# The first chunk of a fused attention and feed-forward kernel rebuilt: two load queues for z, z casts on GpSimd, split z copies, first units squared in halves

## Chip, cores, metric

One NeuronCore of a Trainium2 chip (the sets of rounds ran on four chips; ratios compare runs of one set). The metric is the device time of one execution in microseconds (us). Each figure is the median of several runs. Executions of one program here scatter by about 0.3% (the kernel before: 1205.06 to 1208.82 us in its first four runs), and part of this study is about where that scatter comes from. The record lists a state with every run: those that are compared here are all listed as "fast", or, for a single run, as unknown.

Names of engines: PE is TensorE (PEld its weight loads), DVE is VectorE, ACT is ScalarE, POOL is GpSimd (called Pool below), SP is SyncE.

## The reference

```python
def _attn_ref(u, v, z):                       # u, v: (8, 3008, 256), z: (8, 3008, 64)
    scores = np.matmul(z, z.transpose(0, 2, 1)) / S
    attn = np.maximum(scores, 0.0) ** 2
    return (u * np.matmul(attn, v)).astype(np.float32)

def _moe_ref(x, w_in, w_out):                 # x: (24064, 256), d_ff 2048
    h = x @ w_in
    g = h * (1.0 / (1.0 + np.exp(-1.702 * h)))
    return (g @ w_out).astype(np.float32)     # the kernel's output
```

The attention has no softmax: scores are rectified and squared.

## The kernel before

One batch follows another. For each batch, the 3008 rows are taken in 6 chunks of 512 queries. A *unit* is two blocks of 128 keys against one chunk: two score matmuls into a 128x1024 PSUM tile `sc`, a rectification into `rl`, a square into `a`. An *output step* is one matmul of a V block with half a unit, into one of two accumulators `o`. The first chunk of the first batch has 47 output steps (48 matmuls, since one step has two matmuls of 64 rows); steps 4k to 4k+3 need unit k. Nothing runs ahead of that chunk, so here the whole latency from the first load is bare. Later batches get z by transposing DMAs; the first batch turns z on TensorE instead, in six *turns* of four blocks:

```python
    def first_cast(g):                        # f32 -> f16, written twice (two row halves)
        m = g % CB * CB
        for c in range(2):
            dve.tensor_copy(ZT["st"][g // CB][:, m:m + CB, c, :], ZT["f"][g // CB][:, m:m + CB, :])

    def first_zt(g):
        z2 = ZT["st"][g // CB][:, g % CB * CB:(g % CB + 1) * CB]
        zp = ps1.tile([P, CB, P], F16, name="zp", tag="ps1")       # PSUM
        for k in range(CB):
            pe.transpose(zp[:, k, :], z2[:, k, :, :], ident)
        # ... cut: dst and src views of ZT and zp
        if g in (0, 2, 3):
            act.activation(dst, src, AF.Copy, scale=1.0)
        else:
            dve.tensor_copy(dst, src)
        # ... cut: the odd block of the last turn, copied by VectorE

    def square(b, i, jp, sc):                 # ... cut: forms of later batches
        rl = pw.tile([P, 2, CH], F16, name="rl", tag="rl", bufs=3)
        act.activation(rl, sc, AF.Relu, scale=csc)
        a = pa.tile([P, 2, CH], F16, name="a", tag="a", bufs=21)
        dve.tensor_tensor(a, rl, rl, ALU.mult)
        # ... cut: transposing DMA of a for a later chunk
```

The start of the program, and when units of the first chunk are taken (step: number of units):

```python
    FIRST_ZT = {2: 2, 7: 3, 13: 4, 21: NCH - 1}                  # step: turn
    SCHED0 = {0: {0: 1, 6: 2, 14: 2, 22: 2, 30: 2, 38: 2}, # ... cut: later chunks

    load_v(0, 0, act)                         # V loads; the casts of V run on Pool
    first_z((0, CB, 2 * CB, 4 * CB, NJ))      # all z loads on SP, in four pieces
    for n0 in range(VB, NJ, VB):
        load_v(0, n0, sp)
    warm_up(7)                                # matmuls on nothing
    first_cast(0)
    first_zt(0)
    warm_up(2)
    first_cast(1)
    posts = scores(0, [queue.pop(0) for _ in range(2)])
    first_zt(1)
    posts[0]()                                # a post is one square(...)
    first_cast(2)
    posts[1]()
    first_cast(3)
    take(0, 1)
```

In the traces here each engine works its instructions off in the order of the program: below, a z cast starts at 14.33, right behind the four squares queued ahead of it. A framework adds the semaphore waits from the tiles that the instructions read and write.

## Time and profile before

| | before |
|---|---|
| time, median (range) of the first three runs | 1206.41 us (1205.06 to 1208.82) |
| span of the profiled run | 1203.2 us |
| TensorE busy in 0 to 10, 10 to 20, 20 to 30 us | 6.97, 7.00, 10.00 us |
| first scores | 5.45 us |
| first output matmul | 8.57 us |
| *marker*: first output matmul of the second chunk | 26.91 us |

The page of the profile, its first lines (busy us of each engine, share of the span, instructions):

```profile
span 1203.2 us, 28259 instructions
...
PE 1190.2 (99%) x11785; PEld 715.2 (59%) x11785; DVE 830.5 (69%) x1277; ACT 770.5 (64%) x903; POOL 307.1 (26%) x363
```

Busy time by stretch of the kernel before. The columns are the stretch in us, its length, then each engine's busy us with the number of its instructions, the granted clock of TensorE, the busy share of the DMA engines and GB/s:

```profile
0.00:10.00 10.00, 6.97 (x35) 2.37 (x35) 4.57 (x12) 5.41 (x6) 2.46 (x9) 1.00 0.76 232
10.00:20.00 10.00, 7.00 (x45) 2.73 (x44) 9.06 (x14) 5.94 (x8) 9.77 (x14) 1.00 1.18 277
20.00:30.00 10.00, 10.00 (x52) 3.43 (x51) 7.72 (x11) 7.84 (x9) 2.58 (x4) 1.00 1.23 167
```

TensorE is the limit from 20 us on. Before that it idles 3.03 us in the first stretch and 3.00 us in the second. Of its 6.97 busy us in the first, 3.71 are warm-up matmuls (3.12 and 0.59 us in the timeline), so these are no work either.

The timeline of the kernel before (start us, busy us, engine, line, operation, output and input tiles, shape, count, and in brackets the idle time before with what ended it):

```profile
3.81 0.49 DVE L123 CAST zst<-zf 128x256 f16<-128x256 f32 x2 [2.68 <-DMA zf<-in_z_dram]
...
4.36 0.40 PE L129 MATMUL zp<-ident,zst 128*128 128x128 f16 x4
...
4.80 0.60 ACT L135 ACTIVATE ZT<-zp 128x512 f16<-128x512 f16 x1 [2.26 <-PE zp L129]
...
5.45 0.61 PE L217 MATMUL sc<-ZT 64*128 64x512 f16 x4 [0.26 <-ACT ZT L135]
...
5.88 1.94 ACT L231 ACTIVATE rl<-sc 128x1024 f16<-128x1024 f32 x2 [0.49 <-PE sc L217]
...
7.84 0.68 DVE L245 TENSOR_TENSOR a<-rl 128x1024 f16<-128x1024 f16 x1
...
8.57 0.59 PE L304 MATMUL o<-a,V 128*128 128x512 f16 x2
...
14.33 1.31 DVE L123 CAST zst<-zf 128x256 f16<-128x256 f32 x2
...
15.70 0.40 PE L129 MATMUL zp<-ident,zst 128*128 128x128 f16 x4 [2.35 <-DVE zst L123]
...
24.11 2.33 PE L304 MATMUL o<-a,V 128*128 128x512 f16 x10
...
26.91 1.90 PE L304 MATMUL o<-tt,V 128*128 128x512 f16 x8
```

The chain of the first unit is cast, turn, copy, scores, rectification, square, output. The 2.35 us at 15.70 is the largest wait: a cast of z stands in VectorE's queue behind four squares.

### The profile page before, as it was taken

The page shows a single profiled execution, that of the slowest core. Times are in us where ns is not written, and L with a number is a line of the kernel's source. Part 1 is how long each engine was busy: PE and PEld are TensorE (multiplying, and loading weights), DVE is VectorE, ACT ScalarE, POOL GpSimd, SP SyncE. Part 2 cuts the span into 40 slices and gives each one's busy share as a digit, 9 for nine tenths or more (in the row PEclk, how much of TensorE's full clock was granted, in tenths as well). Part 3 has the DMA queues.
Part 4 walks back from the last instruction along what each step waited for, and adds up shares of the span by engine and source line. Part 5 has one row for each costly group of instructions (what it writes and reads, how often), then busy time and mean ns, then how long its engine had stood idle before and what let it go on. Part 6 is the DMA issues. An engine that isn't in the chain of part 4 may idle for free.

```text
span 1203.2 us, 28259 instructions
## 1 busy us (share of the span) xinstructions
PE 1190.2 (99%) x11785; PEld 715.2 (59%) x11785; DVE 830.5 (69%) x1277; ACT 770.5 (64%) x903; POOL 307.1 (26%) x363
## 2 busy tenths in 40 slices
PE   7999999999999999999999999999999999999998
PEld 2446765467644676446765468554775547844577
DVE  7669954597545976469654696648966489564886
ACT  6777684476844768366683666736677376772764
POOL 4144300352004520044200451015510134101000
PEclk9999999999999999999999999999999999999999
DMA  9966399562994639844399454984459754496012
GB/s 225 169 112 129 114 168 158 86 153 72 169 161 89 151 91 174 159 78 137 94 186 146 80 137 98 194 133 76 138 121 183 133 83 149 114 180 117 1 37 71
DMA packets 366592, 152.33 MB, mean 127 GB/s; under 512 B 313312, under 2 KB 358496, under 8 KB 366464
## 3 DMA queue, kind: packets, MB, share of 16 engines
q1 hardware_dynamic: 330320, 114.08, 48.6%
q0 software_dynamic: 35456, 35.86, 14.8%
q8 instruction: 92, 1.51, 0.5%
q10 hardware_dynamic: 688, 0.59, 0.2%
q14 instruction: 36, 0.29, 0.1%
HBM read 60.29 MB, written 24.64 MB: 71 GB/s over the span
## 4 chain that ended last, share of the span: by engine, by line
PE 95%; DMA 2%; DVE 2%; ACT 1%; issue 0%; SPq 0%; ACTq 0%; DVEq 0%
PE o L304 37%; PE hg L345 26%; PE st L445 17%; PE yp L511 8%; PE sc L217 6%; DMA tt<-a 2%; DVE a L245 1%; ACT rl L231 0%; DMA zf<-in_z_dram 0%; DVE gt L354 0%; DVE zst L123 0%; ACT gf L353 0%; DVE s L416 0%; DVE s L418 0%; PE zp L129 0%
## 5 line engine op out<-in xcount | busy, mean ns | idle before, releaser
L353 ACT ACTIVATE gf<-hg 128x1024 f32<-128x1024 f32 (+1 forms) x384 | 385.8, 1007 | 166.0 <-PE hg L345 138.8
L231 ACT ACTIVATE rl<-sc 128x1024 f16<-128x1024 f32 x311 | 308.1, 1025 | 208.0 <-PE sc L217 205.9
L304 PEld LDWEIGHTS <-V 64*128 64x128 f16 (+1 forms) x4052 | 233.9, 94 | 251.4 <-issue 10.0
L345 PE MATMUL hg<-xt,W 128*128 128x512 f16 (+1 forms) x1408 | 354.5, 374 | 0.1
L354 DVE TENSOR_SCALAR gt<-gf 128x1024 f16<-128x1024 f32 (+1 forms) x384 | 275.5, 718 | 89.0 <-ACT gf L353 84.7
L245 DVE TENSOR_TENSOR a<-rl 128x1024 f16<-128x1024 f16 x276 | 192.0, 697 | 183.8 <-ACT rl L231 181.0
L304 PE MATMUL o<-a,V 64*128 64x512 f16 (+2 forms) x2010 | 316.4, 372 | 0.0
L187 POOL DMA_DIRECT2D uq<-in_u_dram x188 | 129.6, 696 | 509.2 <-PE sc L217 343.5
L304 PE MATMUL o<-tt,V 64*128 64x512 f16 (+1 forms) x1762 | 215.3, 376 | 2.0 <-DMA tt<-a 2.0
L345 PEld LDWEIGHTS <-W 128*128 128x128 f16 x1536 | 141.2, 98 | 117.5 <-issue 0.3
L445 PEld LDWEIGHTS <-gt 128*128 128x128 f16 x2176 | 132.5, 98 | 29.8 <-issue 1.1
L217 PE MATMUL sc<-ZT 64*128 64x512 f16 (+1 forms) x692 | 121.3, 366 | 1.9 <-ACT ZT L135 0.9
L445 PEld LDWEIGHTS <-s 128*128 128x128 f16 x1632 | 99.2, 98 | 20.7
L172 POOL CAST V<-vst 128x512 f16<-128x512 f32 x96 | 90.2, 978 | 65.3 <-DMA vst<-in_v_dram 58.3
L511 PE MATMUL yp<-W,gt 64*128 64x256 f16 x1664 | 104.0, 269 | 0.0
L511 PEld LDWEIGHTS <-gt 64*128 64x128 f16 x1664 | 80.7, 94 | 19.0 <-POOLq L84 4.1
L321 DVE TENSOR_TENSOR xt<-o,ut 128x512 f16<-128x512 f32 x80 | 51.5, 685 | 38.1 <-PE o L304 38.1
L445 PE MATMUL st<-WT,gt 128*128 128x128 f16 x1088 | 71.8, 219 | 0.9 <-ACT uP L455 0.9
L445 PE MATMUL st<-W,gt 128*128 128x128 f16 x1088 | 71.7, 219 | 0.0
L445 PE MATMUL st<-WT,s 128*128 128x128 f16 x1088 | 71.5, 219 | 0.0
L455 ACT ACTIVATE uP<-st 128x256 f32<-128x256 f32 x102 | 39.1, 383 | 38.4 <-DVE y L461 33.7
L217 PEld LDWEIGHTS <-ZT 64*128 64x128 f16 x692 | 37.5, 94 | 37.7 <-issue 6.8
(47 smaller groups left out, 627.3 us busy)
## 6 DMA issues: line engine op xcount, KB each, us to landing
vst<-in_v_dram SPq DMA_DIRECT2D x39, 512.0 KB, 5.0
uq<-in_u_dram POOLq DMA_DIRECT2D x156, 128.0 KB, 3.4
out_dram<-y SPq DMA_DIRECT2D x33, 512.0 KB, 3.7
tt<-a SPq DMA_TRANSPOSE x230, 3.6
uq<-in_u_dram POOLq DMA_DIRECT2D x32, 112.0 KB, 2.9
out_dram<-y POOLq DMA_DIRECT2D x7, 512.0 KB, 5.0
vst<-in_v_dram SPq DMA_DIRECT2D x8, 384.0 KB, 4.5
out_dram<-y POOLq DMA_DIRECT2D x7, 384.0 KB, 4.6
```

The source lines that it names most:

```text
L172: pool.tensor_copy(V16[b][:, n0:n0 + VB, k, :].rearrange("p n (q c) -> p n q c", c=QW), vst.rearrange("p n (q k c) -> p n q k c", k=NCC, c ...
L187: eng.dma_start(uq[k * QW:(k + 1) * QW, :n // QW].rearrange("t q k c -> t q (k c)"), src[:, :, cs])
L217: pe.matmul(sc[:, r, :m * P], zt[h, 2 * kp + r, :], zt[h, (qi + 1) * CB - m:(qi + 1) * CB, :], start=True, stop=True,)
L231: act.activation(rl, sc, AF.Relu, scale=csc)
L245: dve.tensor_tensor(a, rl, rl, ALU.mult)
L304: ins = pe.matmul(acc[c][:, :n], V16[b][h, j, c, :], weights(b, i, j)[h], start=(k, m) == first[c], stop=(k, m) == final[c],)
L321: dve.tensor_tensor(x[:, c, :n], acc[c][:, :n], ut[:, :n], ALU.mult)
L345: pe.matmul(hg[:, e, :n], W1[:, c, ff * P:(ff + 1) * P], XT[b, i][:, c, :n], start=(c == 0), stop=(c == NCC - 1),)
L353: act.activation(gf[:, :, :n], hg[:, :, :n], AF.Gelu_apprx_sigmoid, scale=1.0 / FSC)
L354: dve.tensor_scalar(g, gf[:, :, :n], FSC, None, ALU.mult)
L445: pe.matmul(bank[:, m, :], lhs()[:, f, m, :], right[:, ff, :], start=name in ("P1", "P2", "P5") and m == 0 and ff == 0, stop=ff == NFF // ...
L511: ins = pe.matmul(yp[s // per][:, s % per, :], GT[b, k, ff // CB][h, ff % CB, s * P:(s + 1) * P], W2[h, ff, :], start=new, stop=n == last[ ...
```

## The change

The intent, as its parts show it: bring the second z piece and the first V blocks earlier (z on two queues, V loads reordered), take the z casts off the busy VectorE (to Pool), shorten the first chain by splitting z copies and units between ScalarE and VectorE, and take units every 7 steps, each time with one z turn.

The core of the diff, cut. The new order of loads and of casts on Pool:

```diff
-    load_v(0, 0, act)
-    first_z((0, CB, 2 * CB, 4 * CB, NJ))
-    for n0 in range(VB, NJ, VB):
-        load_v(0, n0, sp)
+    first_z(0, CB, sp)
+    first_z(CB, 2 * CB, act)
+    casts = load_v(0, 0, act)
+    first_z(2 * CB, 4 * CB, sp)
+    for n0 in (VB, 2 * VB):
+        casts += load_v(0, n0, sp)
+    first_z(4 * CB, NJ, sp)
+    for n0 in range(3 * VB, NJ, VB):
+        casts += load_v(0, n0, sp)
+    first_cast(0, pool, 0, 1)
+    for n, cast in enumerate(casts):
+        if n in (0, 4, 8, 9):
+            first_cast((0, 4, 8, 9).index(n) + 2, pool)
+        cast()
     warm_up(7)
+    first_cast(0, dve, 1, 2)
+    first_cast(1, dve)
```

Split copies, halves of units, and the first two units:

```diff
+            act.activation(dst[:, :SREM], src[:, :SREM], AF.Copy, scale=1.0)
+            dve.tensor_copy(dst[:, SREM:], src[:, SREM:])
...
+    def square_halves(jp, sc, r_dve):
+        rl = pw.tile([P, 2, CH], F16, name="rl", tag="rl", bufs=3)
+        a = unit[0, 0, jp] = pa.tile([P, 2, CH], F16, name="a", tag="a", bufs=21)
+        for r in range(2):
+            if r in r_dve:
+                dve.tensor_scalar(rl[:, r], sc[:, r], csc, 0.0, ALU.mult, ALU.max)
+            else:
+                act.activation(rl[:, r], sc[:, r], AF.Relu, scale=csc)
+        for r in range(2):
+            dve.tensor_tensor(a[:, r], rl[:, r], rl[:, r], ALU.mult)
+        turn_unit(0, 0, jp, a)
...
+    FIRST = {7: (2, 3), 14: (2, 4), 21: (2, 5), 28: (2,), 35: (2,), 42: (1,)}   # step: units, turn
+    HALVES = {2: (), 3: (0,), 5: (0,), 7: (0,), 9: (0,)}     # unit: halves rectified by VectorE
...
+    copies = first_zt(2)
+    rls = [pw.tile([P, 2, CH], F16, name="rl", tag="rl", bufs=3) for _ in range(2)]
+    for k, r in ((0, 0), (0, 1), (1, 1)):
+        act.activation(rls[k][:, r], scs[k][:, r], AF.Relu, scale=csc)
+    dve.tensor_scalar(rls[1][:, 0], scs[1][:, 0], csc, 0.0, ALU.mult, ALU.max)
+    for k in range(2):
+        a = unit[0, 0, k] = pa.tile([P, 2, CH], F16, name="a", tag="a", bufs=21)
+        for r in range(2):
+            dve.tensor_tensor(a[:, r], rls[k][:, r], rls[k][:, r], ALU.mult)
+    copies()
```

More of the change, by code (lines that the diff above doesn't have):

```diff
@@ L96, in warm_up @@
             pe.matmul(w, nil[:, :P], nil, start=(k == 0), stop=(k == n - 1))
-    def first_z(cuts):
-        ZT[0] = pz.tile([P, NJ, P], F16, name="ZT", tag="ZT")
-        ZT["st"] = [pa.tile([P, CB * CB, 2, DQK], F16, name="zst", tag="tt", bufs=14) for _ in range(2)]
-        fs = [pw.tile([P, CB * CB, DQK], F32, name="zf", tag="y") for _ in range(2)]
-        for n0, n1 in zip(cuts, cuts[1:]):
-            zf = fs[n0 // (CB * CB)]
-            m0 = n0 % (CB * CB)
-            t0, last = n0 * P, n1 == NJ
-            t1 = (n1 - CB if last else n1) * P
-            sp.dma_start(
-                zf[:, m0:m0 + (t1 - t0) // P, :].rearrange("p (g n) d -> p g (n d)", n=CB),
-                z[0, t0:t1].rearrange("(g p n) d -> p g (n d)", p=P, n=CB),
-            )
-            if last:
-                m1 = m0 + (t1 - t0) // P
-                sp.dma_start(zf[:, m1:m1 + CB - 1, :], z[0, t1:S0].rearrange("(p n) d -> p n d", n=CB - 1))
-                for h in range(2):
-                    sp.dma_start(zf[h * SREM:(h + 1) * SREM, m1 + CB - 1, :], z[0, S0:S])
-        ZT["f"] = fs
@@ L120, in first_cast, with first_z @@
-    def first_cast(g):
+    def first_z(n0, n1, eng):
+        if 0 not in ZT:
+            ZT[0] = pz.tile([P, NJ, P], F16, name="ZT", tag="ZT")
+            ZT["st"] = [pa.tile([P, CB * CB, 2, DQK], F16, name="zst", tag="tt", bufs=14) for _ in range(2)]
+            ZT["f"] = [pw.tile([P, CB * CB, DQK], F32, name="zf", tag="y") for _ in range(2)]
+        zf = ZT["f"][n0 // (CB * CB)]
+        m0 = n0 % (CB * CB)
+        t0, last = n0 * P, n1 == NJ
+        t1 = (n1 - CB if last else n1) * P
+        eng.dma_start(
+            zf[:, m0:m0 + (t1 - t0) // P, :].rearrange("p (g n) d -> p g (n d)", n=CB),
+            z[0, t0:t1].rearrange("(g p n) d -> p g (n d)", p=P, n=CB),
+        )
+        if last:
+            m1 = m0 + (t1 - t0) // P
+            eng.dma_start(zf[:, m1:m1 + CB - 1, :], z[0, t1:S0].rearrange("(p n) d -> p n d", n=CB - 1))
+            for h in range(2):
+                eng.dma_start(zf[h * SREM:(h + 1) * SREM, m1 + CB - 1, :], z[0, S0:S])
@@ L121, in first_cast @@
+    def first_cast(g, eng, c0=0, c1=2):
         m = g % CB * CB
-        for c in range(2):
-            dve.tensor_copy(ZT["st"][g // CB][:, m:m + CB, c, :], ZT["f"][g // CB][:, m:m + CB, :])
+        eng.tensor_copy(
+            ZT["st"][g // CB][:, m:m + CB, c0:c1],
+            ZT["f"][g // CB][:, m:m + CB].unsqueeze(2).to_broadcast([P, CB, c1 - c0, DQK]),
+        )
     def first_zt(g):
@@ L129, in first_zt, with copies, first_take @@
             pe.transpose(zp[:, k, :], z2[:, k, :, :], ident)
-        zt = ZT[0][:, g * CB:(g + 1) * CB, :].rearrange("d n p -> d (n p)")
-        nb = CB if g < NCH - 1 else CB - 1
-        dst = zt[:, :nb * P].rearrange("d (p n) -> d p n", n=nb)
-        src = zp[:, :nb, :].rearrange("d n p -> d p n")
-        if g in (0, 2, 3):
-            act.activation(dst, src, AF.Copy, scale=1.0)
-        else:
-            dve.tensor_copy(dst, src)
-        if nb < CB:
-            dve.tensor_copy(zt[:, nb * P:], zp[:, nb, :])
+        def copies():
+            zt = ZT[0][:, g * CB:(g + 1) * CB, :].rearrange("d n p -> d (n p)")
+            nb = CB if g < NCH - 1 else CB - 1
+            dst = zt[:, :nb * P].rearrange("d (p n) -> d p n", n=nb)
+            src = zp[:, :nb, :].rearrange("d n p -> d p n")
+            act.activation(dst[:, :SREM], src[:, :SREM], AF.Copy, scale=1.0)
+            dve.tensor_copy(dst[:, SREM:], src[:, SREM:])
+            if nb < CB:
+                dve.tensor_copy(zt[:, nb * P:], zp[:, nb, :])
+        return copies
+    def first_take(n, g=None):
+        posts = scores(0, [queue.pop(0) for _ in range(n)])
+        copies = first_zt(g) if g else None
+        posts[0]()
+        if g:
+            copies()
+        for post_ in posts[1:]:
+            post_()
+    def square_halves(jp, sc, r_dve):
[9 more added lines that the diff above has]
+        turn_unit(0, 0, jp, a)
     def load_z(b):
@@ L170, in load_v, with cast @@
                 eng.dma_start(vst[h * SREM:(h + 1) * SREM, full, :], v[b, S0:S])
-        for k in range(NCC):
+        def cast(k):
             pool.tensor_copy(
@@ L175, in load_v, with cast_block @@
             )
+        def cast_block(n):
+            pool.tensor_copy(
+                V16[b][:, n0 + n].rearrange("p k (q c) -> p k q c", c=QW),
+                vst[:, n].rearrange("p (q k c) -> p k q c", k=NCC, c=QW),
+            )
+        if b == n0 == 0:
+            return [lambda n=n: cast_block(n) for n in range(VB)]
+        return [lambda k=k: cast(k) for k in range(NCC)]
     def width(i):
@@ L224, in square @@
     def square(b, i, jp, sc):
+        if b == i == 0 and jp in HALVES:
+            square_halves(jp, sc, HALVES[jp])
+            return
         rl = pw.tile([P, 2, CH], F16, name="rl", tag="rl", bufs=3)
@@ L245, in square, with turn_unit @@
         dve.tensor_tensor(a, rl, rl, ALU.mult)
+        turn_unit(b, i, jp, a)
+    def turn_unit(b, i, jp, a):
         cj = jp // 2
@@ L567 @@
     LOAD = {(3, NJ + 4): 4, (4, NJ + 5): 5}
-    FIRST_ZT = {2: 2, 7: 3, 13: 4, 21: NCH - 1}
+    FIRST = {7: (2, 3), 14: (2, 4), 21: (2, 5), 28: (2,), 35: (2,), 42: (1,)}
+    HALVES = {2: (), 3: (0,), 5: (0,), 7: (0,), 9: (0,)}
     SCHED0 = {
-        0: {0: 1, 6: 2, 14: 2, 22: 2, 30: 2, 38: 2},
+        0: {},
         1: {0: 2, 8: 2, 15: 2, 22: 2, 30: 2, 38: 2},
@@ L589 @@
     fill(0)
-    load_v(0, 0, act)
-    first_z((0, CB, 2 * CB, 4 * CB, NJ))
-    for n0 in range(VB, NJ, VB):
-        load_v(0, n0, sp)
-    warm_up(7)
-    first_cast(0)
-    first_zt(0)
-    warm_up(2)
-    first_cast(1)
-    posts = scores(0, [queue.pop(0) for _ in range(2)])
-    first_zt(1)
-    posts[0]()
-    first_cast(2)
-    posts[1]()
-    first_cast(3)
-    take(0, 1)
+    first_z(0, CB, sp)
[12 more added lines that the diff above has]
+        cast()
+    warm_up(7)
+    first_cast(0, dve, 1, 2)
+    first_cast(1, dve)
+    for copies in [first_zt(g) for g in range(2)]:
+        copies()
+    scs = []
+    for k in range(2):
+        (i, jp), sc = queue.pop(0), ps2.tile([P, 2, CH], F32, name="sc", tag="ps2")
+        for r in range(2):
+            h = slice(r * DQK, (r + 1) * DQK)
+            pe.matmul(sc[:, r], ZT[0][h, 2 * jp + r, :], ZT[0][h, :CB, :], start=True, stop=True)
+        scs.append(sc)
+    copies = first_zt(2)
[3 more added lines that the diff above has]
+    dve.tensor_scalar(rls[1][:, 0], scs[1][:, 0], csc, 0.0, ALU.mult, ALU.max)
+    for k in range(2):
+        a = unit[0, 0, k] = pa.tile([P, 2, CH], F16, name="a", tag="a", bufs=21)
+        for r in range(2):
+            dve.tensor_tensor(a[:, r], rls[k][:, r], rls[k][:, r], ALU.mult)
+    copies()
+    first_take(1)
     load_u(0, 1)
@@ L615 @@
                     load_u(0, 0)
-                if b == 0 and i == 0 and n in FIRST_ZT:
-                    first_zt(FIRST_ZT[n])
-                    if 3 <= FIRST_ZT[n] < NCH - 1:
-                        first_cast(FIRST_ZT[n] + 1)
+                if b == 0 and i == 0 and n in FIRST:
+                    first_take(*FIRST[n])
                 if (i, n) in turn:
@@ L636 @@
             for n0 in range(0, NJ, VB):
-                load_v(b + 1, n0, sp)
+                for cast in load_v(b + 1, n0, sp):
+                    cast()
             fill(b + 1)
```

## The prediction

> **What bounds the kernel now.** The page gives TensorE 99% of 1203.2 us at full clock; the list of busy time by stretch shows it busy 10.00 of every 10 us from 20 us on. Only the head can gain: 6.97 us busy in 0 to 10 us (3.7 of it warm-up matmuls) and 7.00 in 10 to 20. Timeline: first z cast at 3.81, ScalarE's first z copy 4.80 to 5.40, first scores 5.45, first output matmul only at 8.57. Then VectorE limits (9.06 of 10 us busy in 10 to 20): squarings of 1.03 us each beside Pool's V casts, 0.69 alone; TensorE waits 2.35 us at 15.70 for a z cast queued behind four of them. From 8.57 to the 39th output step (26.91 us) I count about 6 us idle.
>
> [...]
>
> **What the change does.**
> - The second z piece goes on ScalarE's queue; V blocks 1 and 2 are issued before the last z. V block 1's cast (now 9.47) comes sooner.
> - Nine of twelve z casts (0.25 us, up to 0.65 contended) leave VectorE; Pool gets four of 0.6 to 0.8 us and a small one, still ending near 17 us.
> - z copies become a ScalarE half (0.38 us by its 256-column form) and a VectorE half (about 0.38 us from its other copies). But in the built program each VectorE half waits for the ScalarE half: about 0.83 us in series, where ScalarE took 0.60.
> - Units 0 to 3, 5, 7, 9 are squared in halves, chained too: unit 1's VectorE half waits for ScalarE's, and unit 0's squarings stand behind it; later ScalarE's half waits for VectorE's (about 0.65 us).
>
> **The sum** (by hand). First scores about 5.8, three ScalarE halves (0.57 each) to 7.85, VectorE half to 8.5, first square 8.9: the first output matmul about 9.0, 0.4 us later than now. Then VectorE has 13.4 us of work up to unit 9, and each second score of a pair waits for ScalarE to empty its buffer: 0.5 to 1 us at steps 14, 21, 28, 35. TensorE's work from first output matmul to the 39th step is about 11.8 us; with waits 15 to 17, so that step comes at 24 to 26 instead of 26.91. Later work is unchanged and TensorE-bound, so the gain stays: about 2 us.
>
> **Predicted: 1204.4 us, 8 in 10 between 1201.8 and 1206.4. Faster by over 2%: 0.003; within 2%: 0.992; slower by over 2%: 0.005.**
>
> **What would show it.** Second z cast at about 4 us instead of 5.71; VectorE z copies just after ScalarE's end; first output matmul at 8.5 to 9.3; the 2.35 us z wait gone; remaining waits of output matmuls and scores below 1.2 us each; TensorE idle in 0 to 30 us about 2 us smaller.
>
> **What would make it wrong.** If the serial halves cost less than I lay out, the first output matmul could come near 7 us and the gain reach 5. If Pool's casts stretch half squares to 0.54 us throughout, the gain vanishes. If TensorE's clock fell in the sparser stretch 5 to 9 us[...], matmuls would take 0.43 us, not 0.22; the 2.35 us gap doesn't do that now.

## More of the kernel before

In the full list of TensorE's work, 38 output matmuls come before 24.11 (in groups of 2, 4, 1, 6, 1, 7, 1, 8 and 8), so the 39th output step is the one at 24.11, and the ten from there complete the 48 of the first chunk.

Who waited for whom on TensorE over the whole kernel before (us in total, times, the longest):

```profile
PE zp L129 <- DVE zst L123: 3.1, 2, 2.4
PE o L304 <- DMA tt<-a: 2.0, 5, 0.7
```

The second line, output matmuls that wait for tiles from the transposing DMAs, lies outside the head.

## The result

| | before | after |
|---|---|---|
| time, median (range), four runs each | 1206.70 us (1205.06 to 1208.82) | 1209.72 us (1207.88 to 1211.19) |
| ratio after / before, 95% interval | | 1.0023 (1.0000 to 1.0047) |
| span of the profiled run | 1203.2 us | 1209.1 us |
| first scores | 5.45 us | 5.49 us |
| first output matmul | 8.57 us | 9.15 us |
| marker | 26.91 us | 29.00 us |

A ratio is the mean time of one kernel's fast runs over that of the other's of the same rounds, so it is not quite the ratio of the medians. The change made the kernel slightly slower, where about 2 us of gain had been predicted. Two more sets of rounds gave 1.0026 (1.0010 to 1.0043) and 1.0020 (1.0004 to 1.0036). The first interval just touches 1, the other two lie above it, so the loss is real, though far within 2%.

The page of the kernel after, and its busy time by stretch, in the same columns:

```profile
span 1209.1 us, 28276 instructions
...
PE 1191.5 (99%) x11783; PEld 716.8 (59%) x11783; DVE 832.2 (69%) x1282; ACT 768.7 (64%) x908; POOL 311.1 (26%) x370
```

```profile
0.00:10.00 10.00, 5.70 (x28) 2.36 (x29) 4.33 (x9) 4.77 (x9) 5.66 (x16) 1.00 0.87 268
10.00:20.00 10.00, 8.97 (x46) 3.33 (x45) 9.09 (x16) 3.58 (x6) 9.54 (x14) 0.83 1.09 242
20.00:30.00 10.00, 8.87 (x45) 3.08 (x44) 8.15 (x16) 7.21 (x10) 1.04 (x2) 1.00 1.23 161
```

TensorE now also idles in 20 to 30 us (1.13 us); VectorE is as full as before in 10 to 20 us, while ScalarE fell from 5.94 to 3.58 us busy: it waits. The granted clock of 0.83 is a mean: the clock records of the trace show one window of 3.41 us from 11.01 at 0.50, and full clock in the rest of the stretch. The output matmuls in the window start 0.43 us apart (13.19, 13.62, 14.05), those after it 0.22 us (14.45, 14.67, 14.89).

The timeline of the kernel after, first unit:

```profile
4.60 0.66 ACT L137 ACTIVATE ZT<-zp 128x256 f16<-128x256 f16 x2 [1.63 <-PE zp L130]
...
5.01 0.75 DVE L138 COPY ZT<-zp 128x256 f16<-128x256 f16 x2 [0.75 <-ACT ZT L137]
...
5.49 0.61 PE L657 MATMUL sc<-ZT 64*128 64x512 f16 x4 [0.71 <-DVE ZT L138]
...
5.92 1.57 ACT L662 ACTIVATE rl<-sc 128x512 f16<-128x512 f32 x3 [0.66 <-PE sc L657]
...
7.53 0.69 DVE L663 TENSOR_SCALAR rl<-sc 128x512 f16<-128x512 f32 x1 [1.76 <-ACT rl L662]
...
8.13 3.12 DVE L667 TENSOR_TENSOR a<-rl 128x512 f16<-128x512 f16 x4
...
9.15 1.25 PE L345 MATMUL o<-a,V 128*128 128x512 f16 x4 [1.71 <-DVE a L667]
```

VectorE's copy starts only when ScalarE's first half is done, and its half rectification (line 663) only after all three of ScalarE's. The first square, which could have begun at about 6.5 us when the first half of `rl` was there, stands behind it at 8.13. Each half square takes 0.78 us (3.12 over 4). So the z that lands earlier (the z casts of turns 0 and 1 are done at 4.26 us instead of 6.75) buys nothing.

The timeline of the kernel after, around the take at step 21. Units 6 (whole) and 7 (halves) are in it:

```profile
17.84 1.03 ACT L269 ACTIVATE rl<-sc 128x1024 f16<-128x1024 f32 x1
...
18.90 0.69 DVE L283 TENSOR_TENSOR a<-rl 128x1024 f16<-128x1024 f16 x1 [0.43 <-ACT rl L269]
18.92 0.39 PE L252 MATMUL sc<-ZT 64*128 64x512 f16 x2 [0.72 <-ACT rl L269]
...
19.51 0.68 DVE L160 TENSOR_SCALAR rl<-sc 128x512 f16<-128x512 f32 x1
...
20.28 0.60 ACT L162 ACTIVATE rl<-sc 128x512 f16<-128x512 f32 x1 [1.42 <-DVE rl L160]
...
20.99 1.03 ACT L269 ACTIVATE rl<-sc 128x1024 f16<-128x1024 f32 x1
...
22.07 0.39 PE L252 MATMUL sc<-ZT 64*128 64x512 f16 x2 [0.60 <-ACT rl L269]
...
25.00 0.39 PE L252 MATMUL sc<-ZT 64*128 64x512 f16 x2 [0.52 <-ACT rl L269]
25.33 1.70 PE L345 MATMUL o<-a,V 128*128 128x512 f16 x7
...
29.00 0.82 PE L345 MATMUL o<-tt,V 128*128 128x512 f16 x3
```

Read it as a loop. ScalarE rectifies a whole unit (1.03 us); VectorE squares it (0.69); only then, in its queue, comes VectorE's half of the next unit (0.68); ScalarE's half of that unit waits for it (0.60 us of work after 1.42 of idle); then comes ScalarE's next whole unit, 3.15 us after the last one (20.99 less 17.84; the round before took 3.63). TensorE needs about 2.4 us for the 7 output steps, the scores of 2 units and a turn in between: 1.61, 0.53 and 0.23 us from start to start where it does not wait (my expectations below say 2.2, which is a little low). So the two engines take turns, neither is full, and TensorE waits to write new scores at 18.92, 22.07 and 25.00. (The fourth of the seven output matmuls from 25.33, at 25.98, is the 39th output step.)

TensorE's waits in the kernel after:

```profile
PE o L345 <- DMA tt<-a: 6.1, 4, 1.9
PE o L345 <- DVE a L667: 2.0, 3, 1.7
PE sc L252 <- ACT rl L269: 1.8, 3, 0.7
```

The wait for z casts (3.1 us before) is gone, as predicted; the second and third lines are new. The first line grew by 4.1 us, but outside the head. That leads to the first question: what of the profiled 5.9 us belongs to the change?

### The 5.9 us taken apart

In all 17 profiles, span less marker less the waits of output matmuls for transposed tiles lies between 1173.8 and 1174.7 us (two examples: before 1203.2 - 26.91 - 2.0 = 1174.3; after 1209.1 - 29.00 - 6.1 = 1174.0). So the profiled difference is 2.1 us of head and 4.1 us of waits for transposes, less 0.3 of remainder. Those waits vary from run to run: the same kernel before showed 2.0 and 6.1 us in two profiles, and the changed kernel 6.1, 6.7 and 4.4. In the profiles nothing else varies as much. The changed kernel's three lie above the mean of the 14 others (3.5 us); whether that too is chance, these profiles cannot tell.

Between these two profiles the head costs 2.1 us, 0.17%. But the size depends on which profile of the kernel before one takes: the second one (before_again, below) has its marker at 28.38, since a half-clock window fell into its head, and against that the change costs 0.6 us. That may even be the common case. The mean clock of a run tells a little about it: 1.000 in the profile without such a window, 0.998 in the one with it. Of the 40 runs of the kernel before whose clock is on record, 5 show 1.000 and 35 show 0.999 or less (0.999 does not settle it: the profile of after, with one such window, and that of act_halves_two_whole, without one, both show 0.999; in before the clock was at half from 1202.21 us, for the last 1.0 us of the run, and the mean is still 1.000). So the loss at the marker is 0.6 to 2.1 us; the three ratios say 2.4 to 3.1 us for the whole. Where the rest comes from is not shown.

### The profile page after: what moved, and what is told of

Same layout as the page of the kernel before. It is cut to its first block, busy times and chain, and to the rows that moved or that the text cites. A ratio compares the mean times of both kernels' runs of the same rounds, so it can differ in the third digit from the quotient of the medians.

```text
span 1209.1 us, 28276 instructions
## 1 busy us (share of the span) xinstructions
PE 1191.5 (99%) x11783; PEld 716.8 (59%) x11783; DVE 832.2 (69%) x1282; ACT 768.7 (64%) x908; POOL 311.1 (26%) x370
## 4 chain that ended last, share of the span: by engine, by line
PE 94%; DMA 2%; DVE 2%; ACT 1%; issue 0%; ACTq 0%
PE o L345 37%; PE hg L386 26%; PE st L486 17%; PE yp L552 7%; PE sc L252 5%; DMA tt<-a 2%; ACT rl L269 1%; DVE gt L395 0%; DVE a L283 0%; PE w L96 0%; ACT gf L394 0%; DVE rl L160 0%; DVE a L667 0%; DVE s L457 0%; ACT rl L162 0%
## 5 line engine op out<-in xcount | busy, mean ns | idle before, releaser
L269 ACT ACTIVATE rl<-sc 128x1024 f16<-128x1024 f32 x304 | 301.5, 1026 | 206.0 <-PE sc L252 204.1
L283 DVE TENSOR_TENSOR a<-rl 128x1024 f16<-128x1024 f16 x269 | 186.2, 693 | 187.2 <-ACT rl L269 184.8
```

## Experiments

Three theories were put up. **S** (serial): the parts of copies and units given to two engines wait on each other, and VectorE has got too much to do. **C** (clock): the sparser stretch makes TensorE's clock fall, and the half clock costs the time. **P** (Pool): Pool's casts beside VectorE stretch the squares. The table has all runs. Half-clock windows are those in the first 30 us, without the start of the program, before the first record of full clock (at 4 to 7 us; at 4.13 in before and 4.19 in after, where the warm-up matmuls until then start 0.43 us apart).

| run | first output matmul | marker | half clock from | waits for transposes | time |
|---|---|---|---|---|---|
| before | 8.57 | 26.91 | none | 2.0 | see above |
| after | 9.15 | 29.00 | 11.01 | 6.1 | see above |
| before_again | 8.63 | 28.38 | 17.09 | 6.1 | ratio 1.0003 (0.9984 to 1.0023) |
| after_again | 9.04 | 28.87 | 8.67 | 6.7 | ratio 1.0026 (1.0010 to 1.0043) |
| act_halves | 7.83 | 24.22 | none | 5.8 | ratio 0.9994 (0.9962 to 1.0027) |
| whole_units | 7.88 | 24.52 | none | 2.7 | ratio 0.9988 (0.9973 to 1.0003) |
| fillers | 9.04 | 28.97 | none | 3.5 | ratio 1.0023 (1.0002 to 1.0045) |
| pool_writes_only | 8.72 | 26.82 | none | 5.0 | 1207.38, one run |
| whole_copies | 8.62 | 27.99 | none | 2.0 | 1206.18, one run |
| casts_on_dve | 8.63 | 29.03 | none | 1.7 | 1206.64, one run |
| swap_halves | 9.12 | 27.04 | 10.88 | 5.4 | 1208.42, one run |
| first_block_whole | 8.67 | 27.79 | none | 3.4 | 1207.00, one run |
| before_queues | 8.54 | 28.99 | 16.58 | 1.5 | 1206.68, one run |
| act_halves_two_whole | 7.59 | 24.02 | none | 4.7 | ratio 1.0004 (0.9982 to 1.0027) |
| swap_and_first_block | 7.95 | 25.45 | none | 1.3 | 1202.91, one run |
| best_again | 7.29 | 24.14 | none | 3.8 | ratio 0.9970 (0.9953 to 0.9988) |
| after_third | 9.17 | 29.02 | 8.66 | 4.4 | ratio 1.0020 (1.0004 to 1.0036) |

Ratios are to the kernel before in the same rounds. All results were correct except pool_writes_only. Its output is wrong, which doesn't matter for the time.

### before_again and after_again: what is noise?

No edit.

> The kernel before once more, as a measure of noise. The marker that I read in every run is the start of the first output matmul of the second chunk (26.91 us in the profile of before, 29.00 after). Every theory: marker 26.7 to 27.1, time ratio 0.998 to 1.002, no half-clock window in the first 30 us. Waits of output matmuls for transposed tiles (2.0 us before, 6.1 us after in the two profiles) may differ by some us if they are chance; if they are a property of the kernel, they stay near 2.

> The changed kernel once more. Marker 28.5 to 29.3 under every theory. If the waits for transposed tiles outside the head are chance, they come out different from 6.1 us and the time ratio is about 1.001 to 1.002 (the head's 2.1 us alone); if they belong to the change, 6 us and 1.004. Theory C (the half clock is a cause): the half-clock window shows up again between 7 and 15 us.

The marker of after came again, to 0.13 us. The marker of before did not: 28.38, not 26.7 to 27.1, because this time a half-clock window opened at 17.09, right after the big wait before 15.53:

```profile
15.53 0.40 PE L129 MATMUL zp<-ident,zst 128*128 128x128 f16 x4 [2.23 <-DVE zst L123]
...
16.62 2.74 PE L304 MATMUL o<-a,V 128*128 128x512 f16 x7
...
28.38 0.82 PE L304 MATMUL o<-tt,V 128*128 128x512 f16 x3
```

The seven output matmuls that took 1.68 us in the first profile take 2.74 here. Both kernels are thus exposed to the clock. The waits for transposes differ by 4.1 us between two profiles of the kernel before (2.0 and 6.1), with no edit; my expectation of a ratio of 1.001 to 1.002 for after_again was too low (1.0026), but its interval holds it. after_third (its expectation stands further below) repeated the marker, 29.02, and the ratio, 1.0020; its remainder of 1173.8 is at the lower edge of what I expected.

### act_halves and whole_units: take the chain between the engines away

act_halves: all halves are rectified by ScalarE, and the first two units go the same way.

```diff
-    HALVES = {2: (), 3: (0,), 5: (0,), 7: (0,), 9: (0,)}
+    HALVES = {0: (), 1: (), 2: (), 3: (), 5: (), 7: (), 9: ()}
...
-    (the block of the first two units, from scs = [] to copies())
+    posts = scores(0, [queue.pop(0) for _ in range(2)])
+    copies = first_zt(2)
+    for post_ in posts:
+        post_()
+    copies()
```

> The changed kernel, halves kept, but every rectifying half of the units given to ScalarE, so that VectorE only squares and no half waits across engines and back. Theory S (the loss is the chain between ScalarE and VectorE, with VectorE overloaded by 0.68 us rectifications): first output matmul at about 7.2 instead of 9.15, marker 25.5 to 27. Theory C (clock): the clock falls again and the marker stays above 28.5. Theory P (Pool's casts stretch VectorE's squares, 0.78 us a half): first output matmul earlier, but marker 27.5 to 28.5 as the squares stay slow.

whole_units: the same, but `HALVES = {}`.

> The changed kernel without any halves of units: rectified whole by ScalarE, squared whole by VectorE, as before the change; z queues, Pool casts, split copies and the new order of takes stay. Theory S: first output matmul about 7.9 (one whole rectification 0.97 and one square 0.7 after scores at 5.5, stretched to about 1 by Pool), marker 25.5 to 27. Theory C: marker above 28.5. Theory P: 27.5 to 28.5. Against act_halves it tells whether halves are worth anything: S gives act_halves a first output matmul 0.5 to 0.7 us earlier.

Markers 24.22 and 24.52: 4.5 to 4.8 us earlier than after, even earlier than S said, and 2.4 to 2.7 us earlier than the kernel before in its better profile. S holds, and P as the main cause falls, as both its ranges are missed by far. C is not settled here: the clock did not fall in these two runs, so they do not separate it from S; fillers and swap_halves do. Halves as such are worth little: act_halves got its first output matmul 0.05 us earlier than whole_units, where S had said 0.5 to 0.7 us. In both runs Pool reads beside VectorE's first squares: the first half square of act_halves took 0.54 us, where it took 0.41 beside Pool's fills (pool_writes_only).

### fillers: is it the clock?

After with 16 more warm-up matmuls on nothing in the gaps (the `if` in the first take holds for the third unit alone):

```diff
     for copies in [first_zt(g) for g in range(2)]:
         copies()
+    warm_up(2)
...
     copies = first_zt(2)
+    warm_up(2)
...
         copies = first_zt(g) if g else None
+        if (0, 0, 2) not in unit:
+            warm_up(6)
...
+                if b == 0 and i == 0 and n in (2, 4, 6):
+                    warm_up(2)
```

> The changed kernel with 16 more warm-up matmuls on nothing in the gaps of the sparse stretch (2 after the first two z turns, 2 after the third, 6 before the first output matmul, 2 each before the third, fifth and seventh output steps), so that TensorE is never sparse from 4 to 11 us. Theory C (the half-clock window is a main cause): no half clock in the first 20 us and marker at 27.5 or less. Theory S: no half clock, but the marker only falls to 28.3 to 28.8, since VectorE and ScalarE set the pace while the clock is low.

The half clock was gone and the marker stayed: 28.97. It even missed S's range by 0.2 us. In this kernel the half clock cost nothing that could be measured. The trace of after shows why: VectorE has no gap of over 0.15 us from 7.53 to 17.4, so all through the half-clock window (11.01 to 14.43) VectorE set the pace. Nor do the added matmuls seem to hide a gain: VectorE's work in fillers runs at the same times as in after, to 0.3 us, and TensorE's last three waits for scores there (at 18.89, 22.04 and 24.97) are as long as in after (0.72, 0.60 and 0.52 us). C falls. In before_again, where TensorE was the limit from 17 us on, the same 3.41 us window came with a marker 1.47 us later.

### pool_writes_only: is it Pool?

```diff
-            pool.tensor_copy(V16[...] , vst[...])      # both forms of the V cast, first batch
+            pool.memset(V16[...], 1.0)
```

> The changed kernel with Pool's V casts of the first batch replaced by constant fills of the same areas (wrong result on purpose): Pool still works and writes, but reads nothing. Theory P (Pool's reads stretch VectorE's squares): half squares at about 0.4 us instead of 0.78, first output matmul about 0.4 us earlier, marker 26 to 27.5. Theory S: squares faster but the chain of rectifications remains, marker 27.8 or more.

The first squares of this run, against those of after (8.13 us, 3.12 us for four):

```profile
8.16 1.42 DVE L667 TENSOR_TENSOR a<-rl 128x512 f16<-128x512 f16 x4
```

Half squares took 0.36 us each, while Pool was filling V blocks (four fills run from 7.45 to 9.37 us). The marker came at 26.82, inside P's range; S had said 27.8 or more. So Pool's V casts, as they run beside VectorE, cost up to 2.2 us in this kernel (29.00 less 26.82). How much of it is the reading alone is not shown: the fills are shorter than the casts and wait for no load, so Pool's z casts come earlier as well, and the run bounds the cost of the V casts as a whole. Squares beside V casts were slow before the change too (1.03 us), so much of this cost is not new; the same test on the kernel before was not run. For the z casts, which the change did move, see casts_on_dve.

### whole_copies and casts_on_dve: the other parts of the change

```diff
-            act.activation(dst[:, :SREM], src[:, :SREM], AF.Copy, scale=1.0)     # whole_copies
-            dve.tensor_copy(dst[:, SREM:], src[:, SREM:])
+            if g in (0, 2, 3):
+                act.activation(dst, src, AF.Copy, scale=1.0)
+            else:
+                dve.tensor_copy(dst, src)
```

> The changed kernel with each z copy whole on one engine again (ScalarE for turns 0, 2 and 3, VectorE for 1, 4, 5). Theory S: first scores at about 5.3 instead of 5.5 to 5.7, marker earlier by 0 to 0.5 us, since the split copies are the smaller part of the chain. If the split were the main part, marker below 27.5.

First scores at 5.18 and marker 27.99: the split copies cost 1.0 us, twice what S had allowed (one run; the marker of the changed kernel itself scatters by 0.15 us).

casts_on_dve: every `first_cast(g, pool)` moved to VectorE, at the places that follow the kernel before (turn 2 after turn 1, the others after each take).

> The changed kernel with all z casts on VectorE again and Pool left to V alone. Theory S (VectorE overloaded): marker at 29.5 or more. Theory P (Pool's reading is what hurts): Pool has fewer reads and frees VectorE, marker below 28.5.

Marker 29.03, no change: both expectations missed. What the casts cost VectorE (0.41 to 0.49 us each) it got back in shorter squares: its first four took 2.25 us instead of 3.12, since Pool, free of z casts, stood idle until 8.50 us, when V landed (the two squares before that took 0.42 us each, the two after it 0.83). But TensorE waited for z casts again, as in the kernel before:

```profile
PE zp L130 <- DVE zst L120: 1.7, 2, 1.1
```

On balance, moving the z casts to Pool was neutral here.

### swap_halves: is it really the loop?

The sharpest test, one edit; which engine takes which half is exchanged:

```diff
-    HALVES = {2: (), 3: (0,), 5: (0,), 7: (0,), 9: (0,)}
+    HALVES = {2: (), 3: (1,), 5: (1,), 7: (1,), 9: (1,)}
```

> The changed kernel with one edit: in units 3, 5, 7 and 9 ScalarE takes the first half and VectorE the second, instead of the other way round. Same instructions, same durations, same engines. Theory S in its sharper form (a loop: ScalarE's whole rectification 1.03, VectorE's square 0.69, VectorE's half rectification 0.68, ScalarE's half 0.60, then ScalarE's next whole one; 3.15 us for every 7 output steps, where TensorE needs about 2.2): ScalarE no longer waits for VectorE, the period falls to about 2.6 us, set by VectorE's own work, and the marker comes at 27.0 to 28.0; the first output matmul stays at about 9.1. If the loop is not the cause, the order of the halves does nothing and the marker stays at 28.8 to 29.1.

The same stretch in swap_halves:

```profile
18.00 0.68 DVE L283 TENSOR_TENSOR a<-rl 128x1024 f16<-128x1024 f16 x1
18.21 0.60 ACT L162 ACTIVATE rl<-sc 128x512 f16<-128x512 f32 x1 [0.61 <-PE sc L252]
...
18.84 0.69 DVE L160 TENSOR_SCALAR rl<-sc 128x512 f16<-128x512 f32 x1 [0.15 <-ACT rl L162]
18.97 1.02 ACT L269 ACTIVATE rl<-sc 128x1024 f16<-128x1024 f32 x1
...
20.58 0.60 ACT L162 ACTIVATE rl<-sc 128x512 f16<-128x512 f32 x1 [0.59 <-PE sc L252]
...
21.08 1.02 ACT L269 ACTIVATE rl<-sc 128x1024 f16<-128x1024 f32 x1
```

ScalarE now waits for scores and not for VectorE; its whole units follow after 2.11 us (21.08 less 18.97) instead of 3.15; over the three rounds of each trace the mean is 2.47 us against 3.24, where I had said 2.6. The marker is 27.04, as expected, with the first output matmul unchanged at 9.12 and the clock window still there. The order of two halves is worth 2.0 us. That the clock window is still there also speaks against C. In the kernel of the change the half that stands behind a square in VectorE's queue comes first, and the free engine waits for it.

### first_block_whole and swap_and_first_block: do the parts add up?

first_block_whole has only the block of the first two units replaced, as in act_halves. swap_and_first_block has both that and the swap.

> The changed kernel with only the first two units whole again (rectified by ScalarE, squared by VectorE); units 3, 5, 7, 9 keep their halves in the order of the change. Theory S: first output matmul at about 7.9 instead of 9.1, but the loop gives part of it back: marker 27.6 to 28.4. If the first block is the whole cause, marker at 24.5 to 25.5 as in whole_units.

> The changed kernel with both cures: halves swapped in units 3, 5, 7, 9 and the first two units whole. If the two chains are the whole loss and add up: marker 24.9 to 26.2 (29.0 less 1.9 for the swap and 1.2 to 2.0 for the first block). If one hides the other: marker above 26.5.

first_block_whole: marker 27.79, in the range, but the first z happened to land late in this run (first VectorE cast at 4.25 instead of 3.43), so the first output matmul was at 8.67 and not 7.9; the 1.2 us gained is probably too low. Both together: 25.45, in the range of the sum. What is left to act_halves (24.22) is probably VectorE's four half rectifications of 0.68 us; no run takes them apart.

### before_queues: the loads alone

The kernel before with the new order of loads only (the `first_z` and `load_v` lines of the first diff above).

> The kernel before with only the new order of loads: second z piece on ScalarE's queue, V blocks 1 and 2 ahead of the last z. Theory S: z cast 2 at about 4.3 instead of 5.71, first output matmul nearly as before (8.2 to 8.6, as unit 0 hangs on the first z piece alone), but VectorE still carries all casts, so the wait for the fifth cast stays in part: marker 25.5 to 26.7. If the loads are the useful part of the change, marker below 25.5.

Inconclusive in size: the second cast was early (four casts done by 4.37 us), but the wait for the fifth cast was still there, 2.73 us, and a half-clock window opened at 16.58, so the marker of 28.99 holds both. Neither the first output matmul (8.54) nor that wait got better, so in this run the loads alone brought nothing. Which parts of the change are the useful ones in whole_units is not shown: the split copies cost 1.0 us, the moved z casts were neutral in the changed kernel, and the takes every 7 steps were not tested alone.

### act_halves_two_whole and best_again: the best version, and does the head reach the end?

act_halves, and the first two z copies whole, one on each engine:

```diff
+            if g < 2:
+                if g == 0:
+                    act.activation(dst, src, AF.Copy, scale=1.0)
+                else:
+                    dve.tensor_copy(dst, src)
+                return
             act.activation(dst[:, :SREM], src[:, :SREM], AF.Copy, scale=1.0)
             dve.tensor_copy(dst[:, SREM:], src[:, SREM:])
```

> Candidate for the best: act_halves, and the first two z copies whole, one on ScalarE and one on VectorE, which can run side by side[...]; later copies split. First scores at about 5.2 instead of 5.7, first output matmul at about 7.4, marker 23.6 to 24.2: 2.7 to 3.3 us before the kernel before's 26.91. The gain should pass to the end: ratio 0.9970 to 0.9985, with chance of 2 us from the waits for transposed tiles.

> act_halves_two_whole once more. If the head's gain of 2.9 us reaches the end: span less marker less the waits of output matmuls for transposed tiles is 1174.3 us plus or minus 0.5, as in every profile so far, and the ratio to the kernel before is 0.996 to 0.999. If later waits take it up, that remainder is larger by some 2 us and the ratio 0.999 to 1.001.

> The changed kernel for the third time. Remainder again 1174.3 plus or minus 0.5, marker 28.8 to 29.1, ratio 1.001 to 1.003; slower than best_again by 3 to 6 us in the means of the same rounds.

The marker is at 24.02 and 24.14, 2.8 to 2.9 us before the kernel before's (in its better profile). That ScalarE and VectorE can read two PSUM tiles side by side is seen in the kernel before, where VectorE's copy out of `zp` (7.23 to 7.93) overlaps ScalarE's rectification out of `sc` (6.80 to 7.82). The first scores (5.48 and 5.39) missed the expected 5.2, and in the first run the first output matmul (7.59) missed 7.4. In the first set of rounds the time did not show it (1.0004, with one run of 1212.22 among six); in the second set it did: 0.9970 (0.9953 to 0.9988), with a median of 1203.40 us, against 1.0020 for the change on the same chip. Against the changed kernel in the same rounds best_again was 5.9 us faster in the mean, inside the 3 to 6 that I had expected. The remainder was 1174.1 and 1174.4 us in the two profiles, so later waits do not take the gain up. Best_again from the first chunk into the second:

```profile
20.09 1.47 PE L351 MATMUL o<-a,V 128*128 128x512 f16 x6
21.79 0.38 PE L351 MATMUL o<-a,V 128*128 128x512 f16 x1 [0.23 <-DVE a L289]
...
24.14 1.90 PE L351 MATMUL o<-tt,V 128*128 128x512 f16 x8
```

One wait of 0.23 us for a square is left in this part. In the second set this version is faster than both kernels, by 0.3% and 0.5%; the first set, against the kernel before alone, shows no difference.

### What stays open

ScalarE's half waits for VectorE's half (1.42 us idle before 20.28 in the kernel after) although they read and write different halves: they share the tiles `sc` (in PSUM) and `rl`. Which of the two the framework orders by is not on record, and whether the order is needed, here or for the halves of a z copy, was not shown. Whether halves that really ran side by side would beat act_halves was not tried.

## Why the prediction was wrong

Predicted 1204.4 us (1201.8 to 1206.4), a gain of about 2 us; measured 1209.72, a loss of 2.1 us in the head between the two profiles, and the rest in waits that vary from run to run. Point by point:

- **First unit.** Predicted: VectorE's copy half after ScalarE's, 0.83 us for the pair; first output matmul about 9.0. Measured: 0.84 us (4.60 to 5.44), and 9.15 (9.04 and 9.17 in the repeats). Right, and S follows from it: the built program shows every such wait before anything runs.
- **The z wait of 2.35 us goes.** Right.
- **Second scores of a pair wait 0.5 to 1 us at steps 14, 21, 28, 35.** Measured 0.72, 0.60 and 0.52 us at 21, 28 and 35, none at 14 (0.3 in the repeats). Right but for the first.
- **The 39th step "comes at 24 to 26".** It came at 25.98. Right at the edge.
- **"instead of 26.91". This is the step that failed.** 26.91 us is not the 39th output step of the kernel before. It is the first matmul of the *second* chunk, the 49th output matmul; the timeline shows it by its input, `tt`, a transposed tile that the first chunk never reads. The 39th was at 24.11 (at 25.58 in before_again, with its half-clock window). I had put the takes of the old schedule one place too late along the timeline. With 24.11 in the sum, the same layout of the changed kernel says a loss of up to 1.9 us, and 1.9 us was measured at that step (25.98 less 24.11); one more unit's pair of score matmuls, taken at step 42, makes it 2.1 at the marker.
- **"I count about 6 us idle" from 8.57 us on.** The same error in another form, and the prediction's own first paragraph refutes it: 7.00 us busy in 10 to 20 us and 10.00 from 20 on leave 3.0 us. Summed over the trace from 8.57 to 26.91 it is 3.0 us. With a headroom of 3.0 us, 0.4 us given away at the start and four waits of 0.5 to 1 us, no gain was left.
- **"If TensorE's clock fell".** It fell, in all three profiles of the changed kernel (from 11.01, 8.67 and 8.66 us). Fillers shows that it cost nothing there. The risk was rightly named and wrongly weighed. The clause that the gap of 2.35 us does not lose the clock held for one profile only: in before_again a gap of 2.23 us did.
- **"If Pool's casts stretch half squares to 0.54 us throughout".** They took 0.78 us at first, 0.42 once Pool was done. As pool_writes_only shows, Pool's V casts as a whole cost at most 2.2 us; as casts_on_dve shows, the z casts that the change gave to Pool cost nothing on balance. What the new order of the V casts cost was not tested alone.

What the prediction did not see as a whole was the loop. It had the two waits (ScalarE's half for VectorE's, scores for ScalarE) but added them up per step, instead of following them round and finding a period of 3.15 us against the 2.4 that TensorE needs.

## What to carry to other kernels

Before you sum a plan against the old timeline, check the anchor: count instructions to it, and see that the idle time you claim to win is there in the busy table. When you split one tile's work between two engines, read the built program's waits first: if one half waits for the other, the split is a chain, and a chain that goes from engine A to B and back to A sets a period (3.15 us here) which no engine's busy share shows. Then let the half that is free to start go first, or leave the work whole on one engine, and judge a change of 2 us by a marker in the trace, not by a time that scatters by 3. Take the marker from more than one profile of each kernel, and look at the clock beside it: one half-clock window moved the kernel before's by 1.5 us.

## What the traces show of the hardware

- **When the clock was halved.** Each of the six half-clock windows in the heads is 3.41 us long. In after it begins two such lengths after the first record of full clock (11.01 less 4.19 is 6.82). I summed TensorE's busy time (transposes counted) over windows of 3.41 us, laid end to end from the start of the full clock, for the head of all 17 profiles. The six windows that were busy for 0.68 to 1.64 us were each followed by a half-clock window; none of those with 1.81 us or more was. So in these runs a window of 3.41 us with less than about half of it busy lost the clock, and it need not be idle throughout. About the same gap, 2.23 and 2.35 us, lost the clock in one profile of the kernel before (before_again) and not in the other, where the two windows over which it falls were busy for 2.39 and 2.08 us.
- **What half clock cost.** In fillers the half clock was taken away and the marker moved by 0.03 us (28.97 against 29.00), VectorE setting the pace; in before_again, where TensorE was the limit, the marker came 1.47 us later with the window (28.38 against 26.91).
- **Squares beside Pool.** 0.78 us a half square beside Pool's casts (after), 0.36 us beside Pool's fills (pool_writes_only). Squares beside Pool's stream of casts took about 1.6 (1.09 against 0.69 us, a whole square in the kernel before) to 2.0 times (0.82 against 0.42, a half square in the kernel after) as long.
- **A split z copy.** Its halves ran one after the other, as the program orders them, and the pair took 0.84 us (4.60 to 5.44 in after) where ScalarE alone took 0.60 (before).
